# Gate rows of a fused FFT-mixer and gated-MLP block made as columns and spread through DRAM, with filter sums and table scaling on GpSimd and the inverse transform two tiles ahead

## The chip, the cores and the metric

The kernel runs on one core of a Trainium2 chip. The metric is the device time of one execution in microseconds (us). The figure of a kernel is the median of its runs, of which one was run under the profiler (the profile of the kernel before is of a further run, 250.93 us). A few timed runs, over 1.5% above the fastest of the same kernel, count as slow; they are in the medians and ranges, but not in the ratios. Engines are named as in the profile: PE is TensorE (matmuls), PEld its weight loads, DVE is VectorE, ACT is ScalarE, POOL is GpSimd, SP is the queue from which most DMAs are issued. SBUF is the memory in which the program's tiles lie, PSUM the one into which its matmuls write.

## The reference

The input is one sequence of 2048 rows of 640 features in bf16, two filter tables of 2048 by 321, the three weights of a gated MLP (640 by 1728, twice, and 1728 by 640), a conditioning row `c` of 640 and modulation weights `w_mod` of 640 by 3840.

```python
mod = (silu(c) @ w_mod).reshape(1, 6, 1, 640)
sa, ca, ga, sb, cb, gb = (mod[:, i] for i in range(6))
h = layernorm(x) * (1 + ca) + sa
x = x + ga * irfft2(rfft2(h) * (w_r + 1j * w_i))     # ga: the first gate row
h = layernorm(x) * (1 + cb) + sb
x = x + gb * ((silu(h @ w_gate) * (h @ w_up)) @ w_down)   # gb: the second gate row
```

The kernel does the transforms as matmuls with tables. It never multiplies by `ga` and `gb` on the data: it multiplies the table of the last inverse transform, `RI`, by `ga`, and the down projection's weights, `Wd`, by `gb`. Each needs the gate row of 640 values in all 128 partitions.

One warning for all that follows. The gate values are small here. Four experiments below put wrong numbers in the first gate row (zero, a row of `w_mod`, or, by a fault of mine, overwritten weights), and the comparison with the reference still called the result correct. So "correct" says nothing of the gate rows, in any run; where I call a gate right, that is by construction.

## The kernel before

The program has a forward transform (16 tiles, to about 36 us), a loop over 21 groups of frequencies (to about 62 us), an inverse transform of 16 tiles (to 82 us), and the gated MLP (to the end, 249 us). The group loop is a pipeline: `stage_a` multiplies a group by a table on TensorE and by the filters on VectorE, `stage_b` and `stage_c` carry it back.

The parts that the change touches, with cuts marked `# ...`:

```python
# gate rows, made in all partitions at once: sc_rep is silu(c), one column block
# per 128 inputs, repeated 128 times, as weights
def mod_bc(j, lo, bank, o=0, ks=range(NC5)):
    gps_ = psum[:, bank, o:o + 320]
    for k in ks:
        nc.tensor.matmul(gps_, lhsT=sc_rep[:, k, :], rhs=wm_r[:, k, j, lo:lo + 320], start=(k == 0), stop=(k == NC5 - 1))
    return gps_
# ...
# the DMA queue SP after the forward transform
t2_dma(0); t2_dma(1); t2_dma(2); t2_dma(3)                    # four transposing DMAs
nc.sync.dma_start(wm_r[:, :, 1:3, :], wm_m[:, :, 1:3, :])     # 1600 KB: sb, cb weights
nc.sync.dma_start(wm_r[:, :, 3, :], wm_m[:, :, 3, :])         # 800 KB: gb weights
nc.sync.dma_start(Htab[:], H_dram)
nc.sync.dma_start(RI[:], RI_dram)
# ...
def stage_a(g):
    # ...
    for c5 in {NG - 4: (0, 1), NG - 3: (0, 1), NG - 2: (2, 3, 4), NG - 1: (2, 3, 4)}.get(g, ()):
        for k in range(NC5):     # sb and cb as columns, with the weights of the 1600 KB load
            nc.tensor.matmul(psum[:, 2 + 2 * (g % 2), 192 + c5:193 + c5], lhsT=wm_r[:, k, 1 + g % 2, 128 * c5:128 * c5 + 128],
                             rhs=sc_col[:, k:k + 1], start=(k == 0), stop=(k == NC5 - 1))
    # ...
# head of the loop: ga in two halves, used as filler for TensorE
ga_mod(320, 5, range(3)); t2_pe(0); t2_pe(1); ga_mod(320, 5, range(3, NC5)); PPs[0] = stage_a(0)
# ...
# end of the loop: gb, and RI times ga on VectorE
nc.scalar.copy(gb_bc[:, 320:640], mod_bc(3, 320, 3, 128))
s1em(0); s1em(1)                      # transforms of inverse tiles 0 and 1
# ... rotations on VectorE
nc.vector.tensor_tensor(RI[:, 0], RI[:, 0], ga_bc[:], ALU.mult)
```

The groups are numbered 0 to 20; NG is 21, so NG-4 is group 17. What matters below is that group NG-4 is the first to read the 1600 KB of weights, and does so 7.5 us after their load is issued.

## Time and profile before

| | before |
|---|---|
| time | 251.58 us, median of 6 runs (250.95 to 251.97) |
| span in the profile | 249.1 us |
| TensorE busy | 243.5 us, 98% |
| VectorE busy | 209.7 us, 84% |
| first filter product of the group loop | 37.81 us |
| first inverse tile on TensorE | 64.75 us |

The next view is the timeline of the SP queue (start in us, duration of the issue, engine, line, operation, output<-input):

```profile
43.81 3.44 SPq L519 DMA_TRANSPOSE rM<-rA  x1
47.30 0.59 SPq L527 DMA_DIRECT2D rM<-in_w_mod_dram  x1
47.93 0.52 SPq L528 DMA_DIRECT2D rM<-in_w_mod_dram  x1
```

The DMA issues of the same stretch (output<-input, queue, count, size, and last the us from issue to landing):

```profile
rM<-in_w_mod_dram SPq DMA_DIRECT2D x1, 1600.0 KB, 7.1
...
rM<-in_w_mod_dram SPq DMA_DIRECT2D x1, 800.0 KB, 9.9
```

So the 1600 KB land at 47.30 + 7.1 = 54.4 us, and the 800 KB at 47.93 + 9.9 = 57.8 us. The timeline of TensorE shows the first use of the 1600 KB, and the start of the inverse:

```profile
54.76 0.39 PE L571 MATMUL psum<-sc_col,rM 128*128 128x1 bf16 x10
...
64.75 0.31 PE L1149 MATMUL psum<-rH,rL 128*128 128x320 bf16 x1
```

Use follows landing by 0.4 us. This is the tightest place of the loop, and nothing on the page says so: a wait of zero leaves no line. The windows view (the stretch and its length, then busy us of PE, PEld, DVE, ACT, POOL, then the clock, the share of the DMA engines' time, and GB/s) shows TensorE full and the DMA at about 400 GB/s there:

```profile
50.00:52.00 2.00, 2.00 (x36) 2.00 (x34) 1.95 (x5) 1.81 (x4) 2.00 (x3) 1.00 1.00 392
...
56.00:58.00 2.00, 2.00 (x49) 2.00 (x46) 1.51 (x4) 1.56 (x3) 1.20 (x2) 1.00 1.03 424
...
60.00:62.00 2.00, 1.91 (x35) 1.73 (x33) 1.95 (x6) 1.69 (x4) 0.15 (x1) 1.00 1.09 367
```

At the head of the loop the timeline of VectorE has the filter sums (line 407) and the first product (line 590):

```profile
35.46 0.95 DVE L407 TENSOR_TENSOR rW<-rW 128x1536 bf16<-128x1536 bf16 x1
...
37.81 0.56 DVE L590 TENSOR_TENSOR rM<-psum,rW 128x384 bf16<-128x384 f32 x1 [0.43 <-PE psum L567]
38.74 0.43 DVE L407 TENSOR_TENSOR rW<-rW 128x512 bf16<-128x512 bf16 x1 [0.37 <-DMA rW<-wflip_r]
```

### The profile page before, as it was taken

To read this page: it belongs to the slowest core of one execution; us is meant where nothing else is said; L and a number is where in the kernel's file an instruction comes from. 1 tells how busy PE (TensorE), PEld (TensorE's weight loads), DVE (VectorE), ACT (ScalarE), POOL (GpSimd) and SP (SyncE) were. 2 spreads that over 40 slices of the span, in tenths; PEclk is the share of its full clock that TensorE was granted. 3 is DMA by queue.
4 is the path that set the end of the run, shared out by engine and by line. 5 is a ranking of instruction groups with operands and counts; after the bars stand their busy time and mean duration, and the time that the engine had idled before them with its cause. 6 is when DMAs were issued, how large, how long until landed. Compare 5 with 4: busy or idle time off the path is not lost.

```text
span 249.1 us, 6473 instructions
## 1 busy us (share of the span) xinstructions
PE 243.5 (98%) x2512; PEld 200.4 (80%) x2512; DVE 209.7 (84%) x524; ACT 162.7 (65%) x300; POOL 74.3 (30%) x122
## 2 busy tenths in 40 slices
PE   8999999999999999999999999999999999999994
PEld 3778877999889888688877778886768887779973
DVE  4798888998898997879997997879995888895895
ACT  3778666997788798488862487674356766235740
POOL 8487755894025422000003900001330000440000
PEclk9999999999999999999999999999999999999999
DMA  7999999999999999300005020003311000211001
GB/s 221 396 357 334 309 365 191 175 397 381 286 352 288 275 264 186 81 9 0 3 0 108 13 68 29 3 3 58 73 42 39 3 0 3 54 53 57 3 0 53
DMA packets 45760, 34.43 MB, mean 138 GB/s; under 512 B 21731, under 2 KB 42658, under 8 KB 45346
## 3 DMA queue, kind: packets, MB, share of 16 engines
q1 hardware_dynamic: 43936, 30.00, 42.8%
q0 software_dynamic: 1504, 3.95, 6.7%
q8 instruction: 19, 0.31, 0.5%
q10 hardware_dynamic: 290, 0.08, 0.1%
q14 instruction: 11, 0.09, 0.1%
HBM read 26.72 MB, written 4.72 MB: 126 GB/s over the span
## 4 chain that ended last, share of the span: by engine, by line
PE 80%; SPq 9%; DMA 6%; ACT 1%; DVE 1%; issue 1%; DVEq 0%; ACTq 0%
PE psum L1016 33%; PE psum L899 19%; PE psum L986 9%; DMA rW<-wflip_r 4%; PE psum L879 3%; PE psum L597 3%; PE psum L664 3%; PE psum L567 2%; SPq L273 2%; SPq L277 2%; PE psum L1149 2%; DMA rM<-in_w_mod_dram 2%; SPq L275 2%; PE psum L1152 2%; PE psum L974 2%; PE psum L618 2%
## 5 line engine op out<-in xcount | busy, mean ns | idle before, releaser
L1016 PEld LDWEIGHTS <-rW 128*128 128x128 bf16 (+1 forms) x528 | 46.9, 98 | 5.6 <-issue 0.2
L1016 PE MATMUL psum<-rW 128*128 128x256 bf16 (+1 forms) x240 | 27.1, 259 | 0.0
L913 POOL TENSOR_TENSOR rM<-rM,rL 128x320 f32<-128x320 f32 x6 | 5.9, 975 | 68.2 <-ACT rL L912 68.2
L899 PEld LDWEIGHTS <-rE 128*128 128x128 f16 (+1 forms) x196 | 19.1, 97 | 7.7
L1016 PE MATMUL psum<-rY,rW 128*128 128x256 bf16 (+1 forms) x96 | 24.0, 259 | 0.0
L986 PE MATMUL psum<-rW 128*128 128x256 bf16 (+1 forms) x170 | 23.1, 291 | 0.0
L899 PE MATMUL psum<-rE 128*128 128x320 f16 (+1 forms) x147 | 22.3, 299 | 0.0
L590 DVE TENSOR_TENSOR rM<-psum,rW 128x384 bf16<-128x384 f32 (+2 forms) x42 | 20.1, 541 | 2.0 <-PE psum L567 1.4
L986 PEld LDWEIGHTS <-rW 128*128 128x128 bf16 x170 | 16.6, 98 | 3.8
L1016 PEld LDWEIGHTS <-rE 128*128 128x128 f16 x192 | 17.4, 98 | 2.4
L899 PEld LDWEIGHTS <-rX 128*128 128x128 bf16 (+1 forms) x151 | 14.6, 97 | 5.4
L760 POOL TENSOR_TENSOR rstd<-rstd,mhalf 128x4 f32<-128x4 f32 (+2 forms) x4 | 4.5, 1120 | 48.2 <-DVE rstd L756 48.2
L1052 DVE TENSOR_TENSOR rH<-psum,rW 128x512 bf16<-128x512 f32 x21 | 14.5, 689 | 4.9 <-PE psum L1016 3.1
L1048 ACT COPY rH<-psum 128x512 f32<-128x512 f32 x21 | 12.3, 585 | 9.0 <-PE psum L1016 7.3
L1042 ACT COPY rW<-psum 128x512 f32<-128x512 f32 x21 | 12.3, 585 | 6.8 <-PE psum L1016 6.7
L1055 ACT COPY rX<-psum 128x512 f32<-128x512 f32 x21 | 12.3, 586 | 6.7 <-PE psum L1016 6.7
L1070 DVE TENSOR_TENSOR rX<-rH,rL 128x512 bf16<-128x512 bf16 x21 | 8.9, 423 | 9.1 <-ACT rL L1068 9.0
L382 DVE SCALAR_TENSOR_TENSOR rE<-rE,mv,psum 128x648 bf16<-128x648 f32 (+1 forms) x17 | 14.2, 844 | 2.1 <-PE psum L318 1.5
L1056 DVE TENSOR_TENSOR rX<-psum,rX 128x512 f32<-128x512 f32 x21 | 14.4, 685 | 1.7 <-ACT rX L1055 1.6
L899 PE MATMUL psum<-rA,rX 128*128 128x320 bf16 (+1 forms) x98 | 15.6, 299 | 0.0
L1016 PE MATMUL psum<-rH,rW 128*128 128x256 f16 (+1 forms) x96 | 15.1, 259 | 0.1
L1016 PE MATMUL psum<-rE,rY 128*128 128x256 f16 (+1 forms) x96 | 15.1, 259 | 0.0
(198 smaller groups left out, 674.3 us busy)
## 6 DMA issues: line engine op xcount, KB each, us to landing
out_dram<-rA SPq DMA_DIRECT2D x31, 80.0 KB, 1.6
rM<-in_w_mod_dram SPq DMA_DIRECT2D x3, 800.0 KB, 9.9
rX<-in_A_x_dram SPq DMA_DIRECT2D x3, 640.0 KB, 7.3
rA<-in_B_w_down_dram SPq DMA_DIRECT2D x2, 960.0 KB, 14.4
rM<-in_w_mod_dram SPq DMA_DIRECT2D x1, 1600.0 KB, 7.1
rY<-in_B_w_gate_dram POOLq DMA_DIRECT2D x2, 768.0 KB, 7.7
rW<-in_B_w_gate_dram SPq DMA_DIRECT2D x2, 640.0 KB, 7.2
rW<-in_B_w_up_dram SPq DMA_DIRECT2D x2, 640.0 KB, 6.5
```

Of the source, the lines that this page charges most:

```text
L382: nc.vector.scalar_tensor_tensor(Zv[:, h], Cv[:, h], mv[:, t, 0:1], zps[:, h], ALU.mult, ALU.subtract)
L590: nc.vector.tensor_tensor(PP[:, :, hl], xv[:, :, hl], in1, ALU.mult)
L597: nc.tensor.matmul(yps[:, i, :], lhsT=_rev(PP, 64 * n * ps + i, [[n, 128]]), rhs=identb[:], start=(ps == 1 and i == 0), stop=(ps == 0 and ...
L899: nc.tensor.matmul(o, lhsT=lhsT, rhs=rhs, start=start, stop=stop, skip_group_check=True)
L986: nc.tensor.matmul(gu[u], lhsT=Wgu[:, u, c5, ff * 128:(ff + 1) * 128], rhs=h2T[:, :, c5, :], start=(c5 == 0), stop=(c5 == NC5 - 1))
L1016: nc.tensor.matmul(o[:, f], lhsT=w, rhs=b, start=(start and f == 0 and i == 0), stop=(stop and f == F - 1 and i == len(ops) - 1), skip_gro ...
L1042: nc.scalar.copy(c0, X)
L1048: nc.scalar.copy(c2, X)
L1052: nc.vector.tensor_tensor(c11, Z, c0, ALU.add)
L1055: nc.scalar.copy(c3, X)
L1056: nc.vector.tensor_tensor(c22, Y, c3, ALU.add)
L1070: nc.vector.tensor_tensor(ato, v4(c11), v4(g21), ALU.mult)
```

## The change

The intent: take the 20 wide matmuls of the gate rows off TensorE (each has 320 columns and gives 128 equal rows), and make each gate row as five columns of 128 values with 25 small matmuls. A column must then become a row in all partitions. The change does that with a store of 1.2 KB to DRAM and a read back that gives every partition the whole row. Four other things change with it: the gate weights are loaded later, two of the filter sums and both table scalings go from VectorE to GpSimd, and the inverse transform runs two tiles ahead in place of one.

The core of the diff (cut: tile declarations, the removed helpers, the transforms of the inverse):

```diff
-    nc.sync.dma_start(wm_r[:, :, 0, :], wm_m[:, :, 0, :])          # ga weights, early
+        nc.sync.dma_start(wm_ga[:], wm_m[:, :, 0, :])              # ga weights, behind the flipped filters
...
-            if t in (13, 15):
-                if t == 13:
-                    wsum(Wn, 48, 64, nc.vector)
-                else:
-                    wsum(Wn, 0, 48, nc.vector)
+            if t == 15:
+                wsum(Wn, 48, 64, nc.vector)
+                wsum(Wn, 0, 32, nc.vector)
+                wsum(Wn, 32, 48, nc.gpsimd)
+                wsum(Wv, 48, 64, nc.gpsimd)
...
-        nc.sync.dma_start(wm_r[:, :, 1:3, :], wm_m[:, :, 1:3, :])
-        nc.sync.dma_start(wm_r[:, :, 3, :], wm_m[:, :, 3, :])
-        nc.sync.dma_start(Htab[:], H_dram)
-        nc.sync.dma_start(RI[:], RI_dram)
+        def g_row(i, eng, row):
+            eng.dma_start(row[:], bass.AP(tensor=g_dram[i].tensor, offset=g_dram[i].offset, ap=[[0, P], [1, D]]))
...
+                    for c5 in {3: (0, 1), 5: (2, 3, 4), NG - 3: (0, 1), NG - 1: (2, 3, 4)}.get(g, ()):
+                        for k in range(NC5):
+                            nc.tensor.matmul(psum[:, 2 + 2 * (g % 2), 200 + c5:201 + c5],
+                                             lhsT=(wm_ga[:, k] if g < 6 else wm_r[:, k, 2]).rearrange("p (m r) -> p r m", r=NC5)[:, c5, :],
+                                             rhs=sc_col[:, k:k + 1], start=(k == 0), stop=(k == NC5 - 1))
             PP = rM.cut(1536 * (g % 4), [3, 2, NT, 2, n])
             prod(g, PP, xps, 0)
-            if g == 0:
-                wsum(Wv, 48, 64, nc.vector)
             prod(g, PP, xps, 1)
+            if g == 5:
+                nc.vector.tensor_copy(gcol[0][:], psum[:, 4, 200:205])
+                nc.sync.dma_start(g_dram[0][:], gcol[0][:])                          # store, 1.2 KB
+                nc.sync.dma_start(wm_r[:, :, 0:2, :], wm_m[:, :, 1:3, :])            # 1600 KB
+                g_row(0, nc.sync, ga_bc)                                             # row, 160 KB
+                nc.sync.dma_start(wm_r[:, :, 2, :], wm_m[:, :, 3, :])                # 800 KB
+                nc.sync.dma_start(RI[:], RI_dram)
+                nc.sync.dma_start(Htab[:], H_dram)
...
-        ga_mod(320, 5, range(3))      # and the two other calls of ga_mod
...
+            if g in (NG - 4, NG - 3):
+                i = NG - 3 - g
+                nc.gpsimd.tensor_tensor(RI[:, i], RI[:, i], ga_bc[:].rearrange("p (m r) -> p r m", r=4), ALU.mult)
...
-        nc.scalar.copy(gb_bc[:, 320:640], mod_bc(3, 320, 3, 128))
         s1em(0)
         s1em(1)
+        s1em(2)
+        nc.gpsimd.dma_start(g_dram[1][:], gcol[1][:])
+        g_row(1, nc.gpsimd, gb_bc)
```

## The prediction

> **What bounds the kernel now.** The windows view shows TensorE busy nearly all of every 10 us from 50 us on; the chain of waits that ends last runs on PE for 80% of the span; VectorE is busy 84%. From 82.4 us to the end (gate/up and down products) the change edits nothing, so it must earn in the first 82 us. Three places there are not bound by PE throughput alone:
>
> 1. 35.9 to 44 us: DMA, then VectorE. The flipped filter lands at 38.65 us, VectorE sums it (0.43 us), then eleven filter products run without a gap (4.88 us).
> 2. 60.6 to 64.75 us, into the inverse: casts, rotation, last forward matmuls and a 0.69 us cast ending at 64.70, which released the first inverse tile. Gate broadcasts (2 x 0.68 us of PE) fill the wait.
> 3. 64.75 to 82.4 us, inverse: 16 tiles at 1.10 us, about 0.4 us of bubbles.
>
> **What the change does.**
> - Removes 20 gate matmuls of 128x320, 0.136 us each: 2.7 us of PE. Adds 50 one-column matmuls: contiguous ones took 23 ns, strided ones at 28 us 32 ns (25 in 0.80 us), so about +1.6 us; net -1.1 us. But half of what goes was filler, and most of the 50 land in PE-bound loops.
> - Moves 800 KB of gate weights behind the flipped filters, which land 1 to 3 us earlier (estimate from 300 to 350 GB/s). With that sum on GpSimd, the second product of group 0 starts about 0.9 us earlier. The gain is then capped: group 5 needs the transposing DMA that landed at about 41.1 us, plus GpSimd's 1.15 us sum. I keep 0.4 us.
> - Gate columns cost about 0.5 us at group 5 and 0.8 us in groups NG-3 and NG-1.
> - Hand-over to the inverse: 0.5 us from splitting tile 0's cast, 0.56 us of tile 2's transform moved into the hole the filler leaves, 0.2 us of bubbles.
> - GpSimd takes two 128x640 table scalings, about 1.45 us each (estimate: 1.15 us for 512 elements, scaled), from VectorE at 0.48. The Trainium skill, "SBUF — State Buffer", section "Who interferes with whom", says a VectorE instruction with two SBUF inputs contends with a GpSimd one that reads SBUF; VectorE's products there read PSUM and SBUF, so I expect little.
>
> **Risks.** The last gate row's weights landed at 57.85 us, uncritical then; now groups NG-3 (about 55.5 us) and NG-1 need them, behind a round trip through DRAM on the same queue. The Trainium skill, "DMA: Bandwidth & Descriptors", section "Anatomy of one DMA", puts about 2.0 us of fixed cost on each DMA; here small edge copies took 5.0 to 5.4 us on GpSimd's queue. A PE stall of 0 to 2 us in NG-3 is the largest uncertainty. GpSimd also waits for the second round trip just before it owes the reciprocal square root at 69.2 us; if late, the inverse slips up to 1 us.
>
> **Sum.** +0.4 -1.3 +1.3 us, less 0.5 us of stall, would be no gain. But the order looks tuned to avoid that stall, and some gate columns should hide: about 1 us better. Predicted 250.6 us, from 248.8 to 252.3. Faster by over 2%: 0.03; within 2%: 0.94; slower: 0.03.
>
> **What would show it.** Right: flipped filter lands by 37 us; second product of group 0 near 38.2; inverse starts 0.5 to 1.5 us earlier and runs without bubbles; after that all only shifted. Wrong: PE idle on the w_mod DMA near NG-3, first inverse tile later than 64.75, VectorE idle on GpSimd near tile 2 or 3, or Wd scaling waiting for the gate row.

## More of the kernel before

The page's busy times (engine, us, share of the span) and its clock row, the granted TensorE clock in tenths over 40 slices:

```profile
PE 243.5 (98%) x2512; PEld 200.4 (80%) x2512; DVE 209.7 (84%) x524; ACT 162.7 (65%) x300; POOL 74.3 (30%) x122
...
PEclk9999999999999999999999999999999999999999
```

TensorE is never long without work, and its clock never falls.

## The result, and the profile after

| | before | after |
|---|---|---|
| time, median of 6 runs each | 251.58 us | 260.82 us (259.10 to 261.63) |
| span in the profile | 249.1 | 259.1 |
| TensorE busy | 243.5 us, 98% | 247.0 us, 95% |
| first product of the group loop | 37.81 | 39.18 |
| first column matmuls of group NG-4 | 54.76 | 59.54 |
| first inverse tile on TensorE | 64.75 | 74.77 |
| first product of the MLP's gate and up weights | 81.28 | 90.47 |

The ratio of the times is 1.036, with a 95% interval of 1.032 to 1.040. Ratios here are the mean time of one kernel's fast runs over the mean of the other's fast runs of the same rounds, so they are not quite the ratio of the medians. The change made the kernel 3.6% slower.

The milestones place the loss: +1.4 us at the head of the loop, +3.4 us more at group NG-4 (4.8 in all), +5.2 us more to the first inverse tile (10.0 in all); the inverse and its hand-over give back 0.8, and the end has it again (10.0). The page shows it as a hole in PE, and a clock that is not at its full value in the same place:

```profile
PE 247.0 (95%) x2542; PEld 204.1 (79%) x2542; DVE 211.3 (82%) x522; ACT 162.0 (62%) x298; POOL 78.9 (30%) x126
...
PEclk9999999997599999999999999999999999999999
```

The timeline of the SP queue:

```profile
47.89 0.54 SPq L585 DMA_DIRECT2D ga_d<-gcol_a  x1
48.49 0.42 SPq L586 DMA_DIRECT2D rM<-in_w_mod_dram  x1
51.81 0.32 SPq L530 DMA_DIRECT2D ga_bc<-ga_d  x1
52.19 0.53 SPq L588 DMA_DIRECT2D rM<-in_w_mod_dram  x1
```

The DMA issues of the stretch:

```profile
rM<-in_w_mod_dram SPq DMA_DIRECT2D x1, 1600.0 KB, 11.0
...
rM<-in_w_mod_dram SPq DMA_DIRECT2D x1, 800.0 KB, 10.0
...
ga_d<-gcol_a SPq DMA_DIRECT2D x1, 1.2 KB, 3.9
```

The store of 1.2 KB (`ga_d<-gcol_a`) takes 3.9 us from issue to landing. The row cannot be issued until then, and the SP queue waits from 48.9 to 51.81 us. The 1600 KB, though issued at 48.49, ahead of that wait, take 11.0 us in place of 7.1, and land at 59.5. The 800 KB land at 62.2 in place of 57.8. The windows:

```profile
50.00:52.00 2.00, 2.00 (x35) 2.00 (x34) 1.80 (x5) 1.78 (x4) 1.98 (x5) 1.00 0.18 22
...
56.00:58.00 2.00, 0.07 (x1) 0.00 (x0) 0.31 (x1) 1.14 (x2) 1.67 (x4) 1.00 1.03 379
58.00:60.00 2.00, 0.46 (x13) 0.47 (x14) 0.00 (x0) 0.00 (x0) 0.42 (x1) 1.00 1.07 380
60.00:62.00 2.00, 0.97 (x22) 0.88 (x19) 1.02 (x2) 0.58 (x1) 0.00 (x0) 0.77 1.07 427
62.00:64.00 2.00, 1.77 (x22) 1.75 (x23) 0.67 (x2) 0.00 (x0) 0.85 (x1) 0.50 0.98 375
```

Compare 50 to 52 us: 392 GB/s before, 22 GB/s now. The weights' data hardly flow until the tiny store has landed. The DMA view of a narrow window, 49.2 to 51.8 us, dates it, first in the kernel before, then in the changed one:

```profile
DMA packets 326, 0.83 MB, mean 321 GB/s; under 512 B 0, under 2 KB 0, under 8 KB 326
```

```profile
DMA packets 20, 0.05 MB, mean 20 GB/s; under 512 B 0, under 2 KB 0, under 8 KB 20
```

The store's own packets, of 10 bytes, are over by 49.2 us, since none under 512 bytes follows, and its landing is at 51.8. In these 2.6 us the load behind it moves 20 packets, and the row is not even issued yet. From 56 TensorE has nothing to do, and from 62 it is busy again but at a clock of 0.50. The waits, in the timeline of TensorE (in brackets the idle time before the group, and what ended it):

```profile
38.60 0.54 PE L568 MATMUL psum<-Ktab,rM 128*128 128x192 bf16 x4 [1.48 <-DVE rM L543]
...
59.54 0.40 PE L572 MATMUL psum<-sc_col,rM 128*128 128x1 bf16 x10 [3.46 <-DMA rM<-in_w_mod_dram]
...
62.23 0.56 PE L577 MATMUL psum<-sc_col,rM 128*128 128x1 bf16 x10 [1.26 <-DMA rM<-in_w_mod_dram]
...
74.77 0.31 PE L1154 MATMUL psum<-rH,rL 128*128 128x320 bf16 x1
```

The first is at the head of the loop and comes from the sums. Those are, on VectorE and on GpSimd:

```profile
35.56 2.79 DVE L408 TENSOR_TENSOR rW<-rW 128x512 bf16<-128x512 bf16 x2
...
39.18 2.88 DVE L602 TENSOR_TENSOR rM<-psum,rW 128x384 bf16<-128x384 f32 x6 [0.43 <-PE psum L568]
```

```profile
35.37 2.43 POOL L408 TENSOR_TENSOR rW<-rW 128x512 bf16<-128x512 bf16 x2
```

Two sums, of 512 and 1536 elements, took 0.42 and 0.95 us on VectorE before (1.37 us). VectorE now sums a quarter less in these two and takes 2.79 us, while GpSimd works on its own two. (The line gives the form of the first of a group; the second has 1024 elements.) The flipped filter landed at 36.3 us in place of 38.65, as predicted, so no sum had to wait for it. Last, the chain of waits that ended last (start, us, what) runs exactly over the store and the loads:

```profile
47.89 3.90 DMA ga_d<-gcol_a
51.81 0.32 SPq L530
...
52.19 10.00 DMA rM<-in_w_mod_dram
```

### The profile page after: what moved, and what is told of

Same layout as the page of the kernel before. It is cut to its first block, busy times and chain, and to the rows that moved or that the text cites. A ratio compares the mean times of both kernels' runs of the same rounds, so it can differ in the third digit from the quotient of the medians.

```text
span 259.1 us, 6546 instructions
## 1 busy us (share of the span) xinstructions
PE 247.0 (95%) x2542; PEld 204.1 (79%) x2542; DVE 211.3 (82%) x522; ACT 162.0 (62%) x298; POOL 78.9 (30%) x126
## 3 DMA queue, kind: packets, MB, share of 16 engines
HBM read 27.05 MB, written 4.72 MB: 123 GB/s over the span
## 4 chain that ended last, share of the span: by engine, by line
PE 79%; DVE 8%; DMA 5%; issue 2%; ACT 2%; POOL 2%; DVEq 0%; SPq 0%; ACTq 0%; POOLq 0%
PE psum L1022 31%; PE psum L905 13%; PE psum L992 8%; DMA rM<-in_w_mod_dram 4%; PE psum L885 3%; PE psum L667 3%; PE psum L609 2%; PE psum L297 2%; PE psum L1154 2%; PE psum L1157 2%; PE psum L568 2%; DMA ga_d<-gcol_a 2%; PE psum L319 1%; PE psum L316 1%; PE psum L336 1%
## 5 line engine op out<-in xcount | busy, mean ns | idle before, releaser
L612 ACT CAST rY<-psum 128x512 bf16<-128x512 f32 (+2 forms) x21 | 11.9, 574 | 13.1 <-PE psum L609 12.9
L766 POOL TENSOR_TENSOR rstd<-rstd,mhalf 128x4 f32<-128x4 f32 (+2 forms) x4 | 4.5, 1122 | 44.1 <-DVE rstd L762 44.1
```

The lines of the kernel that those rows point to most:

```text
L612: nc.scalar.copy(Y2[:, 0:n, :], yps[:, 0:n, :])
```

## The experiments

Seventeen kernels were run. In each table "before" is the kernel before on the same chip.

### 1. Which part of the round trip, and what the clock adds: four changes to the changed kernel

`e1_store_act`: the store goes to ScalarE's queue, so that it does not stand ahead of the weights on SP.

```diff
-                nc.sync.dma_start(g_dram[0][:], gcol[0][:])
+                nc.scalar.dma_start(g_dram[0][:], gcol[0][:])
```

> One line changed against the changed kernel: the 1.3 KB store of the gate columns goes to ScalarE's DMA queue instead of SyncE's. Theory A (in the changed kernel the 1600 KB load of the scale and shift rows, issued 0.6 us after the store on the same queue, moves nothing until the store has landed at 51.8 us): the load starts with the end of the transposes at about 49.2 us and lands near 55 to 56 us instead of 59.5; PE's wait at group NG-4 falls from 3.46 us to under 1 us, the clock stays at 1.0, and the time is 253 to 256 us. The last gate row still waits behind the round trip, so 0.5 to 1.5 us of wait at NG-3 may stay. Rival B (the load is late for its own reasons: transposes, or sharing with the loads after it): it still lands near 59.5, and the time stays within 1 us of 260.8.

`e2_loads_first`: both loads of modulation weights stand ahead of the store.

```diff
         t2_dma(3)
+        nc.sync.dma_start(wm_r[:, :, 0:2, :], wm_m[:, :, 1:3, :])
+        nc.sync.dma_start(wm_r[:, :, 2, :], wm_m[:, :, 3, :])
```

> Against the changed kernel: both w_mod loads (1600 and 800 KB) are issued before the store of the gate columns, the rest keeps its order. Theory A: they land at about 55 and 58 us, no wait at NG-4, up to 1 us at NG-3, clock 1.0. But the store, the row and the two tables now come later, so the table of the inverse may land 1 to 3 us late; time 252 to 255 us. Rival B (the loads are late because the gate columns need them too early, whatever the order): a wait of 3 us or more stays at NG-3, and the time stays over 257 us.

`e3_keep_warm`: the changed kernel with 16 and 4 idle matmuls of 512 columns in the places where TensorE waits, so that its clock stays up. They do no useful work.

```diff
+            for _ in range({NG - 4: 16, NG - 3: 4}.get(g, 0)):
+                nc.tensor.matmul(psum[:, 2 + 2 * (g % 2), :], lhsT=ones[:], rhs=ones[:].unsqueeze(1).to_broadcast([P, 4, 128]),
+                                 start=True, stop=True)
```

> Against the changed kernel: 16 idle matmuls of 512 columns (about 0.22 us each, 3.5 us) at the head of group NG-4 and 4 at NG-3, where PE sat idle for the w_mod loads; nothing else moves, the waits stay. If the granted clock of 0.5 between 61.5 and 71 us comes from PE sitting idle (theory C, the clock gate of the Trainium skill's TensorE page), the clock stays at 1.0, the first inverse tile starts 3 to 5 us earlier than 74.8 us, and the time is 256 to 258 us. If the low clock has another cause (rival D, a throttle by load or chance), the clock stays low in that stretch and the time stays at 260 to 262 us.

`e4_sums_dve`: the filter sums go back to VectorE, in the order of the kernel before.

> Against the changed kernel: the filter sums go back to VectorE as before (48:64 at tile 13, 0:48 at tile 15, the flipped 48:64 between the two products of group 0), nothing on GpSimd at that point. In the changed kernel the two sums of VectorE took 2.79 us together while GpSimd ran its own two (2.43 us); before, 0.42 and 0.95 us. Theory E (the two engines hold each other up): the sum at tile 15 takes about 0.95 us again, the first product of group 0 starts near 37.8 us instead of 39.2, and PE reaches group NG-4 about 1 us earlier. But the loads then land no earlier, so the time gains only 0 to 1.2 us: 259.5 to 261 us. Rival: the sums are long for their shape; then they stay at 0.42 plus 2.3 us.

| kernel | time, us | ratio to before (95%) | before, us |
|---|---|---|---|
| `e1_store_act` | 258.04 | 1.025 (1.018 to 1.033) | 252.18 |
| `e2_loads_first` | 261.95 | 1.039 (1.033 to 1.044) | 252.18 |
| `e3_keep_warm` | 257.78 | 1.022 (1.017 to 1.027) | 252.18 |
| `e4_sums_dve` | 259.13 | 1.030 (1.023 to 1.036) | 252.18 |

In `e1_store_act` the 1600 KB land 8.4 us after issue and TensorE no longer waits for them, but the row still waits for the store (which takes 5.6 us now) and the 800 KB behind it come late: TensorE waits 2.78 us for them, and the clock falls to 0.50 from 61 to 64 us. One move of the store gave back about a third, and 253 to 256 us were expected. (Its profile is of the fastest of its four runs.)

In `e2_loads_first` the 1600 KB land in 7.1 us, as in the kernel before. That is the first sign that the store holds up what follows it. But the store, now behind 2400 KB, takes 9.6 us, SP waits for it until 58.81, and the inverse's tables behind it come late. TensorE waits 3.13 us before the inverse, and the clock falls again; before that it waits 1.23 us for the 800 KB. The loss only moved. I had expected the kernel to gain; it did not.

`e3_keep_warm` did what was expected. The waits are still there, filled with idle work, the clock is 1.00 throughout in the profile, and the kernel is 1.4 percentage points better than the changed one (1.022 against 1.036). It was run at another time. So of the loss, about 3 us is the half clock after the wait, not the wait itself. Its window from 62 to 64 us, where the changed kernel had a clock of 0.50:

```profile
62.00:64.00 2.00, 2.00 (x45) 2.00 (x43) 1.05 (x3) 1.12 (x2) 1.43 (x1) 1.00 0.98 373
```

The Trainium skill explains the halving: "TensorE: Matmul & The Clock Gate", section "What's actually happening", says that the clock gate's default is half rate, and that it returns there after at least one idle window of about 3.4 us. This case's traces agree in kind (1.00 and 0.50, with means between them only in windows that hold a change) but not quite in size: a wait of 2.78 us in `e1_store_act` was enough, and one of 2.13 us in the profile of `e7_best` below was not; and `e5_order` below halves its clock after still shorter waits.

`e4_sums_dve` is 0.6 percentage points better than the changed kernel, with intervals that overlap, and at 259.13 us just under its expected range (259.5 to 261): the sums take 0.95 and 0.42 us again and the first product starts at 37.71 us in place of 39.18. But the loads land no earlier, so the first column matmuls of NG-4 come only 0.36 us earlier (59.18 us against 59.54). The rest of the gain goes with a shorter half clock in its trace (about 59.4 to 66.2 us, against 61.1 to 71.3): the one run of the changed kernel with a mean clock of 0.987 took 259.10 us, and the three runs here with 0.986 took 258.76 to 259.30. What the sums cost in the changed kernel is thus not shown. What is shown is that VectorE's sums take longer beside GpSimd's: 2.79 us in the changed kernel, and 1.85 us for the same two in `e1_store_act`, where GpSimd's second sum had to wait for its data.

### 2. A better order of the queue: three kernels that should have repaired it, and a rival

`e5_order`: both loads, `RI` and `Htab` directly behind the transposes on SP, as in the kernel before; the store (in group 5) and the row (in group 12) on ScalarE's queue; all second-gate columns in NG-1.

```diff
-                g_row(0, nc.sync, ga_bc)
+            if g == 12:
+                g_row(0, nc.scalar, ga_bc)
```

> Against the changed kernel: both w_mod loads and the two tables of the inverse are issued right after the transposes, as before the change; the store and the row of the first gate go by ScalarE's queue; all columns of the second gate are made in the last group NG-1, when its weights (landed 57.9 to 58.7 us in earlier runs) are there. Theory A (the loss is the wait for w_mod data and the halved clock that follows): no PE wait over 0.5 us in the group loop, clock 1.0 throughout, time 251.5 to 254 us. Left of the loss: the contention of the filter sums (0.5 to 1.4 us). GpSimd may hold its rotations back for the table (RI near 59 to 61 us), up to 1 us. Rival F (the change costs through its added matmuls and GpSimd work, not through order): the time stays over 256 us.

`e6_order_sums`: `e5_order` with the sums on VectorE.

> e5 with the filter sums back on VectorE. Theory E (contention of the sums costs 0.5 to 1.4 us at the head of the group loop, and with no wait for data behind it this reaches the end): 0.5 to 1.4 us under e5, 250.5 to 252.5 us. Rival: the sums are hidden, and e6 is within 0.3 us of e5.

`e7_best`: `e6_order_sums` with one table scaling on VectorE, the second trip on ScalarE's queue, and the scaling of `Wd` later.

> e6 with the scaling of table RI taken out of GpSimd's rotations (one half on VectorE as before, the other on GpSimd after the last rotation), the second gate's round trip on ScalarE's queue, and the first five scalings of Wd two tiles later. If what is left of the loss in e6 is GpSimd waiting in its own order for tables and round trips: 249.8 to 251.3 us, so within 1% under the kernel before. Rival: nothing of this is on the path; within 0.4 us of e6.

`b1_two_ahead`: the kernel before with nothing but the inverse transform two tiles ahead, to test the part of the change that I had taken for a gain.

```diff
         s1em(0)
         s1em(1)
+        s1em(2)
...
-            if t and t + 1 < NT:
-                s1em(t + 1)
-                VTs[t + 1] = s1er(t + 1)
+            if t and t + 2 < NT:
+                s1em(t + 2)
+                VTs[t + 2] = s1er(t + 2)
```

> The kernel before with the inverse part of the change alone: three tiles transformed ahead, tile 0's cast split. Gate broadcasts stay, so PE has no hole for the third tile. Theory G (the inverse loses 0.4 to 0.9 us in bubbles between tiles, which running ahead removes): the inverse takes 16.6 to 17.3 us instead of 17.65 after its first matmul, its first matmul comes 0 to 0.6 us later, the time is 250.9 to 251.7 us (0 to 0.5 us faster than before). Rival: the bubbles come from VectorE, and stay.

| kernel | time, us | ratio to before (95%) | before, us |
|---|---|---|---|
| `e5_order` | 257.26 | 1.020 (1.016 to 1.024) | 252.16 |
| `e6_order_sums` | 256.10 | 1.014 (1.010 to 1.019) | 252.16 |
| `e7_best` | 257.42 | 1.023 (1.018 to 1.028) | 252.16 |
| `b1_two_ahead` | 252.26 | 1.000 (0.997 to 1.004) | 252.16 |

`e5_order` missed its expectation (251.5 to 254 us). No wait on TensorE for the weights is left over 0.2 us, but the 1600 KB still take 9.7 us, although they are ahead of everything in their queue, and GpSimd waits 7.54 us for the second store. The wait is gone only because TensorE comes late itself: it waits 1.51 us for the sums at the head, and from about 40.7 to 44.1 us its clock is at 0.50 (the wait in the timeline of TensorE, then the windows):

```profile
38.84 0.54 PE L572 MATMUL psum<-Ktab,rM 128*128 128x192 bf16 x4 [1.51 <-DVE rM L547]
```

```profile
42.00:44.00 2.00, 2.00 (x26) 1.95 (x24) 1.23 (x3) 0.59 (x1) 2.00 (x3) 0.50 1.06 189
```

This fall follows waits of 1.51 and 0.30 us. The changed kernel's profile has waits of 1.48 and 0.30 us in the same places and keeps its clock at 1.00 there, so no single length of wait separates the two.

My theory of the order in the queue was thus only half of it: the trip disturbs the loads from another queue too. The Trainium skill would have told me ("DMA: Bandwidth & Descriptors", section "Issuing engines are not separate DMA queues"): DMAs issued by different engines run on the same 16 DMA engines and interleave. The trace agrees: 9.7 us against 7.1 in the kernel before, with the store on the other queue. `e6_order_sums` is 1.2 us under `e5_order`, the step that was expected of the sums, but misses its own range (250.5 to 252.5 us) by 3.6 us. Nor do the traces show the sums as the cause: the two profiled runs differ the other way (256.57 and 256.86 us), and their first column matmuls come at 58.34 and 58.21 us, when the weights are there. `e7_best` was meant to be the repaired version and was worse than `e6_order_sums`; its 1600 KB land 10.0 us after issue and TensorE waits 2.13 us for them. Its clock held in the profile, but two of its six runs (259.54 and 259.89 us) have mean clocks of 0.985 and 0.987, against 0.999 or 1.0 in the others, so there it fell. `b1_two_ahead` shows no gain at all from the transforms ahead.

### 3. Store, row, or neither

All four kernels of this part are `e6_order_sums` with the trip altered; `e11_pe_bcast` also makes the first gate's columns in one group and reads the gate weights contiguously. Three give wrong gate rows.

`e8_no_trip`: no store and no row for the first gate; the row is zero.

```diff
-                nc.scalar.dma_start(g_dram[0][:], gcol[0][:])
-            if g == 12:
-                g_row(0, nc.scalar, ga_bc)
+        nc.gpsimd.memset(ga_bc[:], 0.0)
```

> The kernel e6_order_sums without the first trip through DRAM at all: no store of the gate columns, no row read, the first gate row set to zero (wrong result on purpose). Theory D (the trip disturbs the big weight loads, by the store or by the row): the 1600 KB load lands 7 to 7.5 us after its issue as in the kernel before (9.4 in e6), no wait of PE for it over 0.5 us, 252 to 253.5 us. Rival E (something else in the changed loop delays the load, the order of the issues or the transposes' tail): the load still lands 9 us or more after its issue, and the time stays 255 to 257 us.

`e9_row_only`: no store; the 128 reads of one row stay, but read a row of `w_mod`.

```diff
-                nc.scalar.dma_start(g_dram[0][:], gcol[0][:])
             if g == 12:
-                g_row(0, nc.scalar, ga_bc)
+                nc.scalar.dma_start(ga_bc[:], bass.AP(tensor=wm_v.tensor, offset=wm_v.offset, ap=[[0, P], [1, D]]))
```

> e6_order_sums without the store; the row of 1280 bytes is still read 128 times from one place in DRAM, a row of the modulation weights, at the same point of the program (wrong result on purpose). If the store is what slows the loads (D1): the 1600 KB load lands 7 to 7.5 us after issue and the time is that of e8 within 0.7 us. If the 128 reads of one place are it (D2): it lands 9 us or more after, and the time is within 0.7 us of e6 (256.1).

`e10_spread_rows`: the store stays; the row is read from 128 different rows of `w_mod` (a step of 3840 where `e9_row_only` has 0).

> e6_order_sums with the store kept, and the row read from 128 different places (the same 128 packets of 1280 bytes, from 128 rows of the modulation weights; wrong result on purpose). D1 (store): as e6, load +9 us or more, 255.5 to 256.7 us. D2 (reads of one place): load lands within 7.5 us, time as e8, 252 to 253.5 us. The row itself takes under 1 us of packets here if reading one place is slow, against about 3 us in e6.

`e11_pe_bcast`: no trip for either gate. A gate column, repeated as weights, times the identity gives the row in all partitions: five matmuls of 128 columns, 0.44 us in the timeline, and a copy from PSUM.

```diff
+        def g_bcast(i, views):
+            for c5, v in enumerate(views):
+                nc.tensor.matmul(v, lhsT=gcol[i][:, c5:c5 + 1].to_broadcast([P, 128]), rhs=identb[:], start=True, stop=True)
...
+            if g == 5:
+                g_bcast(0, [psum[:, 3, 128 * c:128 * c + 128] for c in range(4)] + [psum[:, 5, 256:384]])
+                nc.scalar.copy(ga_bc[:, 0:512], psum[:, 3, :])
+                nc.scalar.copy(ga_bc[:, 512:640], psum[:, 5, 256:384])
```

> Right result: e6_order_sums with both gate rows spread over the partitions by TensorE (five matmuls of 128 columns, the gate column broadcast as weights against the identity) and copied by ScalarE or VectorE, no trip through DRAM. If the DRAM trip is what costs (theory D): the loads land as in e8, no wait for the second row at the hand-over, GpSimd has no wait over 4 us for gb_d, 251.5 to 253.5 us, level with the kernel before. If the gate columns themselves, or the transforms two ahead, cost (rival): 254 us or more.

| kernel | trip of the first gate | 1600 KB land after | wait of TensorE for them | time, us | ratio to before (95%) |
|---|---|---|---|---|---|
| `e6_order_sums` (above) | store, one row 128 times | 9.4 us | 1.64 us | 256.10 | 1.014 (1.010 to 1.019) |
| `e10_spread_rows` | store, 128 rows | 9.8 us | 1.71 us | 256.52 | 1.019 (1.012 to 1.027) |
| `e9_row_only` | one row 128 times | 8.6 us | 1.78 us | 255.73 | 1.015 (1.009 to 1.021) |
| `e8_no_trip` | none | 7.3 us | 0.47 us | 254.95 | 1.012 (1.007 to 1.017) |
| `e11_pe_bcast` | none (nor of the second) | 7.1 us | none | 253.73 | 1.008 (1.003 to 1.014) |

The kernel before had 252.56 us in the call of the last four. The landing times, from the DMA issues of `e6_order_sums` and then of `e11_pe_bcast`:

```profile
rM<-in_w_mod_dram SPq DMA_DIRECT2D x1, 1600.0 KB, 9.4
```

```profile
rM<-in_w_mod_dram SPq DMA_DIRECT2D x1, 1600.0 KB, 7.1
```

The landing times settle that the trip is what delays the loads: without it they are back at 7.1 and 7.3 us (7.8 in `e12_bcast_first` below, also without a trip), with either half of it they are not. Neither of my two narrow theories met its numbers. With the store alone to blame, `e9_row_only` should have landed at 7.0 to 7.5 us and took 8.6; with the row alone, `e10_spread_rows` should have, and took 9.8. By these single landings both halves disturb, and they do not add up; `e10_spread_rows` still reads 128 rows, and no kernel with the store alone was run. The halves also act at different times. In `e9_row_only` the rate dips where the one row is read 128 times, and in `e10_spread_rows`, which reads as many bytes at about that point from 128 places, it does not (windows view, last column GB/s, first `e9_row_only`, then `e10_spread_rows`):

```profile
54.00:55.00 1.00, 1.00 (x19) 0.90 (x16) 1.00 (x3) 0.99 (x3) 1.00 (x2) 1.00 0.98 239
55.00:56.00 1.00, 0.10 (x2) 0.00 (x0) 0.34 (x1) 1.00 (x2) 0.92 (x2) 1.00 0.70 170
```

```profile
54.00:55.00 1.00, 1.00 (x18) 1.00 (x16) 0.95 (x3) 1.00 (x2) 1.00 (x3) 1.00 1.02 410
55.00:56.00 1.00, 1.00 (x19) 0.88 (x16) 1.00 (x3) 0.99 (x3) 1.00 (x2) 1.00 1.05 393
```

That dip is one execution's: `e6_order_sums` also reads one row 128 times, and from 53 us its rate is never under 322 GB/s up to 60 us. With the store, the rate is low earlier, as the loads set in: 39, 232 and 264 GB/s in `e6_order_sums` in the three us from 50 to 53, and 72, 320 and 397 in `e8_no_trip`, whose loads are issued at the same time (48.8 us). Why a store of 1.2 KB holds back a load of 1600 KB is not settled by these runs; only that it does, and in the changed kernel between its last packet and its landing. The times are less clear than the landings, since the intervals of `e6_order_sums`, `e8_no_trip`, `e9_row_only` and `e10_spread_rows` overlap; `e9_row_only` is 0.8 us over `e8_no_trip`, about the scatter. `e8_no_trip` itself missed its range (252 to 253.5 us) by 1.5 us: the first trip is not all that was left.

`e11_pe_bcast` missed its range (251.5 to 253.5) by 0.2 us. It is 1.2 us under `e8_no_trip`, which still has the second trip and in which GpSimd waits 7.1 us for the second store to land. That is about what the second trip costs there; the intervals of the ratios overlap, and `e11_pe_bcast` differs in its columns too. What remained over the kernel before showed in an odd line of VectorE, beside the table scaling on GpSimd (timelines of the two engines in `e11_pe_bcast`):

```profile
61.59 1.34 DVE L707 TENSOR_SCALAR one_p_cb<-modcols 128x5 f32<-128x5 f32 x1
62.84 1.21 DVE L652 CAST rE<-psum 128x1024 bf16<-128x1024 f32 x1
```

```profile
61.48 1.42 POOL L710 TENSOR_TENSOR rH<-rH,ga_bc 128x640 bf16<-128x640 bf16 x1
```

Adding 1 to five columns took 1.34 us; the same took 0.17 us in the kernel before. It ends when GpSimd's scaling ends (62.9 us). The cast after it (line 652) was late for that, and TensorE waited 0.80 us for the cast.

### 4. The trip alone in the good kernel, the sums alone, and the end of the repair

`b2_trip`: the kernel before with the store of 1.2 KB, the row read and the queue order of the changed kernel, and nothing else.

```diff
+        nc.sync.dma_start(g_d[:], sc_col[:])
         nc.sync.dma_start(wm_r[:, :, 1:3, :], wm_m[:, :, 1:3, :])
+        nc.sync.dma_start(wm_r[:, 0, 0, :], bass.AP(tensor=g_d.tensor, offset=g_d.offset, ap=[[0, P], [1, D]]))
         nc.sync.dma_start(wm_r[:, :, 3, :], wm_m[:, :, 3, :])
-        nc.sync.dma_start(Htab[:], H_dram)
         nc.sync.dma_start(RI[:], RI_dram)
+        nc.sync.dma_start(Htab[:], H_dram)
```

> The kernel before, with nothing of the change but a trip through DRAM in its DMA queue: a store of 1.2 KB, then the 1600 KB load, the row read back into all partitions (into a place that nothing reads), the 800 KB load, inverse table, Htab, as the changed kernel has them. Theory D+C (the trip delays the loads; the idle PE then runs at half clock): 1600 KB load lands at 57 to 60 us (54.4 before), a wait of PE for it of 2 to 5 us at the fourth group from the end, then clock 0.5 for some us: 256 to 259.5 us. If the columns of the gate, the sums or the transforms ahead are the larger part (rival): under 254 us.

`b3_pool_sums`: the kernel before with the sums of the changed kernel.

> The kernel before, with nothing of the change but the filter sums moved (two on VectorE and two on GpSimd after the last forward tile). If two engines reading SBUF at once slow each other: the two sums on VectorE take 1.8 to 2.8 us together against 0.42 and 0.95, the first product starts 0.5 to 1.5 us later, 252.5 to 254 us. If the move is a gain as I predicted: 251 to 252 us.

`e12_bcast_first`: `e11_pe_bcast` with two small things moved.

```diff
-                nc.vector.tensor_scalar_add(one_p_cb[:], modcols[:, 3, :], 1.0)
+                nc.vector.tensor_scalar_add(one_p_cb[:], psum[:, 4, 192:197], 1.0)
...
+        g_bcast(1, ...)
         s1em(0)
         s1em(1)
         s1em(2)
-        g_bcast(1, ...)
```

> e11_pe_bcast with two small things moved: the five spreading matmuls of the second row stand before the first inverse transforms, where PE waited 0.80 us, and the addition of 1 to five columns reads PSUM in place of SBUF (it took 1.34 us beside GpSimd's table scaling, 0.17 in the kernel before). If SBUF sharing made it long, it now takes 0.2 us and the wait of PE at the hand-over falls from 0.80 to under 0.4; 252 to 253.3 us, level with the kernel before or 0.5 us above; below 251.5 I don't expect. If it stays over 0.8 us, sharing is not its cause.

`b4_trip`: `b2_trip` with the row read into a tile that is free at that time, and the calls standing in group 5 of the program.

```diff
-        nc.sync.dma_start(wm_r[:, 0, 0, :], bass.AP(tensor=g_d.tensor, offset=g_d.offset, ap=[[0, P], [1, D]]))
+                nc.sync.dma_start(gb_bc[:], bass.AP(tensor=g_d.tensor, offset=g_d.offset, ap=[[0, P], [1, D]]))
```

> b2_trip repeated without its fault (there the row was read into a place that the next products on TensorE read, and they waited 22 us for it): the kernel before, with nothing of the change but the store of 1.2 KB, the row read back and the order of the DMA queue that the changed kernel has; the row goes into a tile that is free until the hand-over. Theory D+C: the 1600 KB load lands at 57 to 60 us (54.4 before), PE waits 2 to 5 us for it at the fourth group from the end, then half clock for some us: 256 to 259.5 us. Rival (columns, sums, transforms ahead are the larger part): under 254 us.

`e13_cols_at_head`: `e12_bcast_first` with the first gate's weights loaded early again, and its columns made at the head of the loop.

```diff
+        ga_col((0, 1))
         t2_pe(0)
         t2_pe(1)
+        ga_col((2, 3))
```

> e12_bcast_first with the first gate's weights loaded as early as in the kernel before, and its 25 column products moved from the fourth group into the head of the group loop, where PE waits 0.36 + 0.30 us. If those waits are filled: 251.4 to 252.4 us, 0 to 0.8 us under e12 (252.5), level with or just under the kernel before. If the earlier load delays the flipped filter (it landed at 38.65 us in the kernel before) by more than the waits: 252.5 to 253.5 us.

| kernel | time, us | ratio to before (95%) | before, us |
|---|---|---|---|
| `b2_trip` | 274.40 | 1.087 (1.081 to 1.093) | 252.16 |
| `b4_trip` | 258.75 | 1.026 (1.022 to 1.031) | 251.96 |
| `b3_pool_sums` | 253.69 | 1.005 (1.000 to 1.011) | 252.16 |
| `e12_bcast_first` | 252.51 | 1.000 (0.996 to 1.004) | 252.16 |
| `e13_cols_at_head` | 253.30 | 1.007 (1.004 to 1.010) | 251.96 |

`b2_trip` was a faulty experiment. I had put the row where the next gate products on TensorE read, and earlier in the program than they, so TensorE waited 22.08 us for the row. It says nothing on the question, and its first gate is wrong.

`b4_trip` answers it. With no part of the change but the trip and the queue order, the good kernel loses 6.8 us, and its trace repeats the changed kernel's: the store takes 4.1 us, the 1600 KB take 11.1, TensorE waits 4.72 us for them, and the clock halves. First the wait on TensorE, then the windows:

```profile
59.51 0.42 PE L568 MATMUL psum<-sc_col,rM 128*128 128x1 bf16 x10 [4.72 <-DMA rM<-in_w_mod_dram]
```

```profile
50.00:52.00 2.00, 2.00 (x36) 2.00 (x34) 1.95 (x5) 1.81 (x4) 2.00 (x4) 1.00 0.13 10
...
56.00:58.00 2.00, 0.00 (x0) 0.00 (x0) 0.00 (x0) 0.00 (x0) 1.14 (x2) 1.00 1.03 365
...
62.00:64.00 2.00, 2.00 (x23) 1.99 (x21) 1.02 (x2) 0.65 (x2) 0.00 (x0) 0.50 0.95 374
```

The 10 GB/s from 50 to 52 us are there too, without gate columns, without GpSimd's sums and without the transforms ahead.

`b3_pool_sums` is 1.3 us slower in its mean. It does not isolate what it should: the sums on VectorE took 1.83 us in place of 1.37, but the sum of the flipped filter, on GpSimd, also came later than on VectorE (39.38 us, taking 1.14 us), and TensorE waited 1.91 us. The move is not a gain, and whether sharing or the slower engine is the larger part is left open.

`e12_bcast_first` shows the last piece. The five-column addition that took 1.34 us now reads PSUM, and takes 0.15 us beside the very same scaling on GpSimd (timelines in `e12_bcast_first`):

```profile
61.68 0.15 DVE L707 TENSOR_SCALAR one_p_cb<-psum 128x5 f32<-128x5 f32 x1
```

```profile
61.45 1.43 POOL L710 TENSOR_TENSOR rH<-rH,ga_bc 128x640 bf16<-128x640 bf16 x1
```

The wait of TensorE at the hand-over fell from 0.80 to 0.35 us, by this and by the five matmuls moved, and the kernel is level with the kernel before. The Trainium skill has this: "SBUF — State Buffer", section "Who interferes with whom", says that VectorE's second pair of SBUF ports is the one that GpSimd uses, that it is an exclusive lock, and that a `tensor_scalar` can take both pairs, and then one engine blocks the other for a whole instruction. The trace agrees: 1.34 us from SBUF, 0.15 from PSUM.

`e13_cols_at_head` tried to beat the kernel before and missed. Its columns did stand in the old waits, but the copy of the columns (on ScalarE) shares a PSUM bank with the next group, and TensorE waited 0.82 us for that copy. No version beats the kernel before; `e12_bcast_first` equals it.

## Why the prediction was wrong, point by point

I predicted 250.6 us (248.8 to 252.3), "within 2%" with 0.94; it was 260.82. The step that failed is in the prediction's own sum: "less 0.5 us of stall, would be no gain. But the order looks tuned to avoid that stall". I had named the stall and its place, group NG-3, and then argued it away by what the order of the code seemed to intend.

- The stall, "0 to 2 us in NG-3". Measured: 3.46 us in NG-4 and 1.26 us in NG-3, 4.7 us together. I looked only at the 800 KB, which the change needs earlier. I did not ask what the store does to the 1600 KB ahead of them, since those are issued before the row and do not wait for it. They landed 11.0 us after issue in place of 7.1. In the kernel before, their use followed their landing by 0.4 us, so there was no room for that; the prediction never read this distance. `b4_trip` shows that the trip and the queue order alone do it; `e8_no_trip` and `e11_pe_bcast` show it gone without the trip.
- The cost of a small DMA. I reckoned with about 2.0 us of fixed cost on each DMA, after the Trainium skill ("DMA: Bandwidth & Descriptors", section "Anatomy of one DMA"); the section gives that figure for DMAs issued from GpSimd, and the first trip is on SP. The first gate's stores of 1.2 KB took 3.9 us in the changed kernel, 4.1 in `b4_trip`, 5.6 to 6.2 on ScalarE's queue, and 9.6 behind 2400 KB of loads. The edge copies of 5.0 to 5.4 us, which I had read in the trace and quoted, were the better guide.
- The clock. The prediction has no word on it. TensorE ran at 0.50 from about 61.1 us, between the two waits, to 71.3. `e3_keep_warm` puts this at about 3 us (1.4 points of ratio). Idle time can be paid twice.
- "+0.4" at the head, from the earlier flipped filter and a sum on GpSimd. Measured: the filter landed 2.3 us earlier, as I had it, but the first product came 1.4 us later. The two sums on VectorE took 2.79 us beside GpSimd's two. In the kernel before, the same move cost 1.3 us in the mean (`b3_pool_sums`); in the changed kernel the wait for the weights takes the lateness up, so a cost there is not shown. I had costed only what VectorE loses in work. I had applied the rule on shared SBUF ports to the table scaling and dismissed it there, and did not apply it to the sums, which have two SBUF inputs on both engines at once.
- "I expect little" from the table scalings beside VectorE's products. Those products read one input from PSUM, and are not slowed (0.54 us on average before and after), so the argument for the products holds. But a five-element addition took 1.34 us beside a scaling in `e11_pe_bcast` (0.99 in `e5_order`), and `e12_bcast_first` shows the cause. In the changed kernel itself the addition fell clear of the scaling and took 0.17 us.
- The hand-over, "0.5 us from splitting", "0.56 us of tile 2's transform moved", "0.2 us of bubbles". In the changed kernel the stretch from the first inverse tile to the first gate/up product is 15.7 us against 16.5 (90.47 - 74.77 and 81.28 - 64.75), so about 0.8 us is there. It is moved rather than gained: `b1_two_ahead` has it alone, its stretch is as short (66.57 to 82.32 us), its first tile comes later, and it gains nothing.
- "-1.3" for the gate columns and "net -1.1 us" of TensorE work. These were small and of about the right kind: `e12_bcast_first`, which keeps the columns and the rest but the sums, the trips and the order of the DMA queue, is level with the kernel before. That the whole idea has no gain to give was right in the prediction ("would be no gain"); what it missed is what the trip costs.

What the account leaves over: the late part, from 90 us to the end, costs 0.8 us more than before, and one VectorE operation of 896 elements there took 1.36 us at 146.56 in place of 0.61, beside GpSimd's work. That the shifted phase of the two engines causes it is argued, not tested.

The first trip with the queue order, its stall and its half clock, make 6.8 of the loss of 9.2 us (`b4_trip`). It was run at another time. How the other 2.4 us divide is not shown, and the costs of single pieces elsewhere can't be added to it. The sums: the first column matmuls come at 59.51 us in `b4_trip` and at 59.54 in the changed kernel, so the 1.4 us lost at the head are gone in the wait. The second trip: in the changed kernel GpSimd waits 5.53 us for the second store, but then another 2.48 us for VectorE. What the traces do show is the stretch from those matmuls to the first inverse tile, 15.2 us against 12.4 in `b4_trip`: it holds the wait of 1.26 us for the 800 KB, which `b4_trip` does not have, and about 10 us at half clock in place of 6.

## What to carry to other kernels

Before putting a small store and a read back into a DMA queue, read for each large load of that stretch how long before its first use it lands: 0.4 us of room is none, and the profile page shows no line for a wait that is zero. A value that must go from a column to all partitions is cheaper by a matmul against the identity (0.44 us here, and 0.86 us of copies on ScalarE) than through DRAM, where a store of 1.2 KB took 3.5 to 9.6 us and delayed its neighbours. An idle time of TensorE can cost twice, once as a wait and once as half clock: a wait of 2.78 us did it here, and once waits of 1.51 and 0.30 us did. And a small VectorE operation beside a long GpSimd one should read PSUM if it can (0.15 us here in place of 1.34).

## What the Trainium skill lacked or had wrong

- "DMA: Bandwidth & Descriptors", section "Anatomy of one DMA": about 2.0 us of fixed cost. The stores of 1.2 KB from 128 partitions to DRAM took 3.5 to 9.6 us here (3.5 in `e3_keep_warm`, 9.6 in `e2_loads_first`). The section's fit is for DMAs issued from GpSimd; no figure is there for small stores under load on the SP and ScalarE queues.
- The same page has nothing on a core's own small store holding back a large load behind it or beside it: 1600 KB took 10.0 to 11.1 us behind the store on one queue, 8.4 to 10.0 us with the store on another queue, and 7.1 to 7.8 us without a trip.
- The same page, section "Rules for kernel authors", allows a source to repeat, as in reading one row into all partitions, and gives no cost: with it the DMA rate fell from 412 to 239 and 170 GB/s for two us (`e9_row_only`), and did not fall when 128 different rows were read (`e10_spread_rows`); `e6_order_sums`, with the same kind of row, shows no such dip (322 at the lowest), so the cost stays open.
- "TensorE: Matmul & The Clock Gate", section "What's actually happening": at least one idle window of about 3.4 us before the clock halves. Here a wait of 2.78 us did it (`e1_store_act`, clock 0.50), and in `e5_order` waits of 1.51 and 0.30 us within 3.3 us did; single waits of 1.64 to 2.13 us did not in the profiles of `e6_order_sums` and `e7_best`.
- "SBUF — State Buffer", section "Who interferes with whom", was right, and has no sizes for operations like these: two sums with two SBUF inputs took 2.79 us beside GpSimd's, against 1.37 us for a third more elements before, and a five-element `tensor_scalar` took 1.34 us in place of 0.17.
